# 136 columns in the weighted sums by differences of logits, an earlier count, and two kv steps one period later

## The chip, the cores and the metric

The kernel runs on one core of a Trainium2 chip. The metric is the device time in microseconds of one launch. The engines that matter here are TensorE (PE, matrix products), VectorE (DVE), ScalarE (ACT), GpSimd (POOL) and SyncE (SP), whose queue issues nearly all DMAs.

## The reference

Two layers follow one another: attention over a pooled key-value image, and a mixture of eight low-rank adapters, of which each token takes the best two. There are 4 batches of 12,288 tokens with 128 channels.

```python
kv_pool = kv.reshape(B, H // r, r, W // r, r, C).mean(axis=(2, 4))     # r = 4: 768 keys a batch
k = v = kv_pool.reshape(B, -1, C) @ w_sr
a = softmax(q @ k.T / sqrt(C))
x = (a @ v).reshape(B * S, D)

logits = x @ w_gate                                    # E = 8
topk = np.argpartition(-logits, 2, axis=1)[:, :2]
w = softmax(logits[topk])
out = x + sum(w[k] * (x @ A[topk[k]]) @ B[topk[k]])    # rank 16
```

Which two adapters are taken and their weights depend on differences of logits alone.

## The kernel before

**Tiling.** The 49,152 tokens are 96 chunks (NCH) of 512, 24 (CPB) to a batch. A chunk is 4 groups (NS) of 128 tokens, and a batch's 768 keys are 6 blocks (NJ) of 128. Two chunks are a pair.

**One chunk's way.** `scores` (L310) makes exp(scores) in three rounds: two products of 512 columns on PE into a score bank (L318, tile sg, two banks in turn), and one exponential on ACT (L319, tile tt). `weigh` (L321) multiplies them with the values: 24 products in two halves of 12, each with its own weight load of tt and as moving operand a row block of `vext` (L330, tile xps). A row of vext has VW = 137 columns: 128 value channels, the values times w_gate (8 logits, linear as the sum is), and a one, which gives the softmax's denominator. `normalise` (L334) takes the denominator's reciprocal (L337, kept in `rinv_all`), multiplies all 137 columns by it (L341, tile xn), and takes the sorted largest 8 of each token's logits (L348). xn is half of a tile that holds a pair, from a pool of five such tiles (`xpool`). `gate` on POOL (L350, five small instructions a pair) turns logits and largest two into tanh arguments, ACT takes the tanh, `send_gates` writes them to device memory by way of SP's queue (L418), and `load_gates` (L425) fetches them back broadcast over 128 partitions. Meanwhile PE transposes xn (L397, tile t_ps), DVE copies it (L408, xt), PE multiplies by A (L432, h_ps), DVE multiplies with the fetched gates (L435, ht), PE multiplies by B (L478, d_ps), DVE adds xn (L492, osb), and SP sends a pair (L510).

**Periods.** The whole order is written out by hand. A loop over c from 2 to 94 (L675) makes one period each: three rounds of scores for chunks ahead, `weigh(c-1)` in two halves, `normalise(c-1)`, the transposes of chunk c-2, and for chunks `lag` periods back (9 at first, then 8, 7 and from chunk 81 on 6) the product with A, and one period later the product with B and the output. Where the lag falls by one, one period handles two chunks. Engines work in program order, so what stands ahead in a queue delays what stands behind.

**Keys and values of the next batch.** `plan` (L270) spreads the work for batches 1 to 3 over the periods: loads of kv in 12 pieces, sums of rows and columns on POOL (L185, L189, L190), and three steps of three parts each: `pooled_transposed` (two transposes of the sums, L201), two periods later `values` (L205, products with `wext`, the 128 columns of w_sr and 8 of w_sr times w_gate), one later `keys` (L213). For batch 1 the steps begin in periods 9, 13 and 19; the sums they need are issued in periods 3 to 6, 8 to 10 and 12 to 16. `squares` and `ranges` (L251, L262) sum the values' squares on POOL and DVE, the latter in periods 32, 40, 56 and 80.

**The check of the ranges.** The kernel counts, over all tokens, denominators that lie in a safe range, and decides at the end by a flag whether a slow exact path (L905) must run. The first CUT = NCH - 8 = 88 chunks are counted by DVE in periods 89 to 91 (`count_ok`, L539), the values' ranges in period 92 (`values_ok`), and PE, ACT and DVE form the sum in period 93 (`count_sum`). In each of these periods the instruction stands in DVE's queue between L348 and L435. The other 8 chunks are counted by POOL after the last output addition (`tail_ok`, L562), on which one product (L569), a sum and the flag (L570, L572) follow.

Of the kernel before, what the change touches and what calls it, by code (L numbers as in the profile page):

```python
# [10 lines left out]
FP32 = mybir.dt.float32  # L11
# [4 lines left out]
AF = mybir.ActivationFunctionType  # L16
ALU = mybir.AluOpType
AX = mybir.AxisListType
# [3 lines left out]
def kernel(  # L22
# [10 lines left out]
    nc = tc.nc  # L33
    P = 128
    B, N, C = q.tensor.shape
    E = 8
# [3 lines left out]
    NJ = NKV // P  # L40
    NTOK = 512
    NS = NTOK // P
    VW = C + E + 1
    CPB = N // NTOK
    NCH = B * CPB
    scale = 1.0 / float(np.sqrt(C))
# [4 lines left out]
    const = ctx.enter_context(tc.tile_pool(name="const", bufs=1))  # L51
    kvpool = ctx.enter_context(tc.tile_pool(name="kvpool", bufs=4))
    keep = ctx.enter_context(tc.tile_pool(name="keep", bufs=1))
    qpool = ctx.enter_context(tc.tile_pool(name="qpool", bufs=3))
    ttpool = ctx.enter_context(tc.tile_pool(name="ttpool", bufs=4))
    xpool = ctx.enter_context(tc.tile_pool(name="xpool", bufs=5))
    run = ctx.enter_context(tc.tile_pool(name="run", bufs=3))
    small = ctx.enter_context(tc.tile_pool(name="small", bufs=3))
    ps_t = ctx.enter_context(tc.tile_pool(name="ps_t", bufs=1, space=bass.MemoryType.PSUM))
# [3 lines left out]
        name="ps_x", bufs=1, side="right", space=bass.MemoryType.PSUM))  # L63
# [90 lines left out]
    w_sr_sb = const.tile([P, P], FP32)  # L154
# [3 lines left out]
    wext = const.tile([P, C + E], FP32)  # L158
# [6 lines left out]
    mm(wg_ps, wT, w_gate_sb, start=True, stop=True)  # L165
    nc.vector.tensor_copy(wext[:, C:C + E], wg_ps)

    gw_all = keep.tile([P, 4, E, 2 * NS], F16, name="gw_all")
    rinv_all = keep.tile([P, NCH, NS], FP32, name="rinv_all")
    vss = keep.tile([P, 2 * B], FP32, name="vss")  # L170
    kpT, kfT, vext, sqsum = {}, {}, {}, {}
    kp_keep = keep.tile([P, B, NKV], FP32, name="kp_keep")
    for b in range(B):
        kpT[b] = kp_keep[:, b]
        if b >= 2:
            kfT[b], vext[b] = kfT[b - 2], vext[b - 2]
# [3 lines left out]
        nc.vector.memset(vext[b][:, :, C + E:VW], 1.0)  # L180


    def sum_row(b, t, d, eng):
# [8 lines left out]
    def stile(name):  # L192
        return ps_s.tile([P, 2, NTOK], FP32, tag="sg", name=name)
# [9 lines left out]
        nc.scalar.activation(kpT[b][:, 2 * t * P:2 * (t + 1) * P], kp_ps, AF.Copy)  # L203

    def values(b, t):  # L205
        v_ps = stile("v_ps")[:, 0, 0:2 * (C + E)].rearrange("p (g e) -> p g e", g=2)
        for g in range(2):
            j = 2 * t + g
            mm(v_ps[:, g], kpT[b][:, j * P:(j + 1) * P], wext, start=(g == 0), stop=(g == 1),  # L209
               skip_group_check=True)  # L210
        nc.scalar.activation(vext[b][:, 2 * t:2 * t + 2, 0:C + E], v_ps, AF.Copy)

    def keys(b, t):  # L213

# [23 lines left out]
            nc.vector.tensor_copy(kfT[0][:, k], k_ps)  # L238

    def tile_values(t):  # L240
        v_ps = mtile([P, 2, C + E], name="v_ps")
        for g in range(2):
            j = 2 * t + g
            mm(v_ps[:, g], kpT[0][:, j * P:(j + 1) * P], wext, start=(g == 0), stop=(g == 1),
               skip_group_check=True)
        if t < NT - 1:
            nc.scalar.activation(vext[0][:, 2 * t:2 * t + 2, 0:C + E], v_ps, AF.Copy)
        else:
            nc.vector.tensor_copy(vext[0][:, 2 * t:2 * t + 2, 0:C + E], v_ps)

    def squares(b, t):  # L251

        v = vext[b][:, 2 * t:2 * t + 2, 0:C + E]
        sq = keep.tile([P, 2, C + E], FP32, name=f"sq{b}") if t == 0 else small.tile(
            [P, 2, C + E], FP32, tag="sq", name="sq", bufs=1)
        nc.gpsimd.tensor_tensor(sq, v, v, op=ALU.mult)
        if t == 0:
            sqsum[b] = sq
        else:
            nc.gpsimd.tensor_tensor(sqsum[b], sqsum[b], sq, op=ALU.add)  # L260

    def ranges(b):  # L262
        nc.vector.tensor_reduce(vss[:, b:b + 1], sqsum[b][:, :, 0:C], axis=AX.XY, op=ALU.add)
        nc.vector.tensor_reduce(vss[:, B + b:B + b + 1], sqsum[b][:, :, C:C + E], axis=AX.XY,
                                op=ALU.add)


# [2 lines left out]
    def plan(b):  # L270
        c0 = CPB * (b - 1)
        if b == 1:
            at = [2, 2, 3, 4, 5, 5, 6, 8, 9, 9, 11, 13]
            sm = [3, 5, 6, 8, 9, 10, 12, 14, 16]
            st = [9, 13, 19]
        else:
            at = [-11, -9, -7, -5, -5, -3, -1, 1, 1, 3, 5, 7]
            sm = [-3, -1, 1, 3, 5, 7, 9, 11, 13]
            st = [4, 10, 16]
        for i, k in enumerate(at):  # L280
            loads.setdefault(c0 + k, []).append((b, i // 4, i % 4))
# [23 lines left out]

    tt, xps, xpair, xn, gw, gin, xT, hg, hgT, hps = {}, {}, {}, {}, {}, {}, {}, {}, {}, {}
    garg = {}
    GRP = GROWS // NTOK

    def scores(c, r):  # L310
# [10 lines left out]
    def weigh(c, h, banks=None):  # L321
# [5 lines left out]
        for j in range(h * NH, (h + 1) * NH):  # L327
            for s in range(NS):
                o = xps[c][:, s // 2, (s % 2) * VW:(s % 2 + 1) * VW]
                mm(o, tt[c][:, j, s * P:(s + 1) * P], vext[b][:, j, 0:VW],  # L330
                   start=(j == 0 and s % 2 == 0), stop=(j == NJ - 1 and s % 2 == 1),
                   skip_group_check=True)

    def normalise(c):  # L334
        ri = rinv_all[:, c]
        xv = xps[c][:, :, 0:2 * VW].rearrange("p b (s v) -> p b s v", v=VW)
        nc.vector.reciprocal(ri.rearrange("p (b s) -> p b s", b=2), xv[:, :, :, VW - 1])  # L337
        if c % 2 == 0:
            xpair[c // 2] = xpool.tile([P, 2 * NS, VW], FP32, tag="xn", name="xn")
        xn[c] = xpair[c // 2][:, (c % 2) * NS:(c % 2 + 1) * NS]  # L340
        nc.vector.tensor_tensor(  # L341
            xn[c].rearrange("p (b s) v -> p b s v", b=2), xv,
            ri.rearrange("p (b s) -> p b s", b=2).unsqueeze(3).broadcast_to([P, 2, 2, VW]),
            op=ALU.mult)
        if c % 2 == 0:
            gin[c // 2] = small.tile([P, 2 * NS, 8], FP32, tag="top", name="top")
        for s in range(NS):
            nc.vector.max(gin[c // 2][:, (c % 2) * NS + s], xn[c][:, s, C:C + E])  # L348
# [287 lines left out]
    warm(2)  # L636
    scores(0, 1)
    tile_values(1)
    scores(1, 1)
    weigh(0, 0)  # L640
# [16 lines left out]

    NQ = NCH // GRP

# [15 lines left out]
    for c in range(2, NCH - 1):  # L675
        b, k = divmod(c, CPB)
# [24 lines left out]
        prep_step(c)  # L701
        if c == CUT + 5:
            count_sum(0)
# [40 lines left out]
        name="ps_e", bufs=1, reuse_waits="tile", space=bass.MemoryType.PSUM))  # L744
# [57 lines left out]
    q_ = n // 2  # L802

    top = small.tile([P, 2 * NS, 8], FP32, tag="top", name="top")
    top4, top5 = top[:, 0:NS], top[:, NS:2 * NS]
    pair = xpool.tile([P, 2 * NS, VW], FP32, tag="xn", name="xn")
    xn[n - 1], xn[n] = pair[:, 0:NS], pair[:, NS:2 * NS]
    arg4, msk4, arg5, msk5 = (
        small.tile([P, NS, E], FP32, tag=f"r{i}", name=f"r{i}", bufs=1) for i in range(4))
    def tops4(c, top, y):  # L810
        ri = rinv_all[:, c]
        xv = y[:, :, 0:2 * VW].rearrange("p b (s v) -> p b s v", v=VW)
        nc.vector.reciprocal(ri.rearrange("p (b s) -> p b s", b=2), xv[:, :, :, VW - 1])
        nc.vector.tensor_tensor(
            xn[c].rearrange("p (b s) v -> p b s v", b=2), xv,
            ri.rearrange("p (b s) -> p b s", b=2).unsqueeze(3).broadcast_to([P, 2, 2, VW]),
            op=ALU.mult)
        for s in range(NS):
            nc.vector.max(top[:, s], xn[c][:, s, C:C + E])
# [11 lines left out]
        name="ps_f", bufs=1, side="right", space=bass.MemoryType.PSUM))  # L831
# [73 lines left out]
    with tc.If(bad_v != 0):  # L905
# [4 lines left out]
        e = big2[:, 0:NKV]  # L910
# [115 lines left out]
```

## Time and profile before

| | us |
|---|---|
| three runs | 378.99, 379.06, 381.55 |
| median | 379.06 |
| profiled execution | 378.6 |
| its span, first to last instruction | 376.8 |
| DVE busy in it | 300.4 |
| ACT busy in it | 310.1 |

In the profile, a row of a group names line, engine, operation and tiles, then busy time and mean duration, then the engine's idle time just before and what ended it. In a timeline the columns are start, duration, engine, line, operation, tiles, count, and in brackets the idle time before with its releaser. A matmul's duration there includes the way through the array; the distance between starts is what it costs in a stream. In the chain of waits the columns are start, duration, engine, tile and line.

### The profile page before, as it was taken

The numbers are of one execution on the slowest core, as the hardware profiler recorded it, in microseconds if no ns is written. First come the engines' busy times: TensorE is split into PE (matmuls) and PEld (weight loads), VectorE is DVE, ScalarE is ACT, GpSimd is POOL, SyncE is SP. The second block draws the span as 40 slices with busy tenths as digits, with TensorE's granted clock in tenths as the row PEclk, the third lists the DMA queues.
The fourth block names the chain that finished last, engine by engine and source line by source line (L and its number), as shares of the span: only waits on it lengthen the run. The fifth ranks groups of instructions, "written<-read, shape, count | busy, mean of one in ns | idle before, by whom it ended". The sixth has DMA issues, their size and how long they took to land.

```text
span 376.8 us, 10584 instructions
## 1 busy us (share of the span) xinstructions
PE 359.5 (95%) x3943; PEld 265.0 (70%) x3943; DVE 300.4 (80%) x950; ACT 310.1 (82%) x391; POOL 225.1 (60%) x375
## 2 busy tenths in 40 slices
PE   4889999999999999999999999999999999999983
PEld 1446767777777677777777777777776767776772
DVE  3784557888888788788888888888888898889983
ACT  1569999898898898988988898898888888888752
POOL 1013799979699887755679687755434234242244
PEclk9999999999999999999999999999999999999998
DMA  8998999999999999999999999998788699654325
GB/s 260 402 363 202 307 295 331 319 285 303 286 341 318 273 293 328 232 312 317 301 294 370 289 313 308 234 305 262 235 221 259 201 257 242 184 141 142 115 85 198
DMA packets 95593, 101.00 MB, mean 268 GB/s; under 512 B 58804, under 2 KB 59060, under 8 KB 95540
## 3 DMA queue, kind: packets, MB, share of 16 engines
q1 hardware_dynamic: 94068, 100.11, 94.5%
q8 instruction: 31, 0.51, 0.6%
q10 hardware_dynamic: 1472, 0.20, 0.3%
q14 instruction: 22, 0.18, 0.2%
HBM read 62.33 MB, written 25.90 MB: 234 GB/s over the span
## 4 chain that ended last, share of the span: by engine, by line
PE 78%; DVE 7%; POOL 7%; DMA 4%; issue 1%; ACT 1%; ACTq 0%; SPq 0%; POOLq 0%; DVEq 0%
PE xps L330 32%; PE sg L318 28%; PE d_ps L478 5%; PE t_ps L397 5%; PE h_ps L432 4%; DMA b_f<-in_moe_B_dram 3%; POOL kvt L185 2%; DMA kvt<-in_kv_dram 2%; DVE xn L341 2%; DVE ht L435 1%; PE v_ps L209 1%; DVE kvt L185 1%; POOL q L107 1%; POOL kvt L189 1%; PE kp_ps L201 1%
## 5 line engine op out<-in xcount | busy, mean ns | idle before, releaser
L319 ACT ACTIVATE tt<-sg 128x1024 f16<-128x1024 f32 x288 | 277.6, 1022 | 37.9 <-PE sg L318 37.0
L318 PE MATMUL sg<-qT,kfT 128*128 128x512 f16 x576 | 170.1, 379 | 0.4 <-ACT qT L585 0.3
L330 PEld LDWEIGHTS <-tt 128*128 128x128 f16 x2304 | 147.7, 98 | 28.5 <-DVE xn L341 18.6
L330 PE MATMUL xps<-vext,tt 128*128 128x137 f16 x2256 | 166.5, 223 | 0.3 <-DVE xn L341 0.2
L492 DVE TENSOR_TENSOR osb<-d_ps,xn 128x512 f32<-128x512 f32 x85 | 58.7, 691 | 30.0 <-PE d_ps L478 29.7
L357 POOL TENSOR_TENSOR arg<-xn,top 128x64 f32<-128x64 f32 x47 | 14.7, 313 | 102.0 <-DVE top L348 86.2
L341 DVE TENSOR_TENSOR xn<-xps,rinv_all 128x548 f32<-128x548 f32 x94 | 68.4, 728 | 3.3
L318 PEld LDWEIGHTS <-kfT 128*128 128x128 f16 x576 | 49.2, 98 | 24.1 <-issue 0.6
L185 POOL TENSOR_TENSOR kvt<-kvt 128x1024 f32<-128x1024 f32 x27 | 63.6, 2357 | 2.6 <-PE sg L318 2.5
L107 POOL CAST q<-q 128x1024 f16<-128x1024 f32 x45 | 46.8, 1041 | 24.8 <-DMA q<-in_q_dram 24.6
L435 DVE SCALAR_TENSOR_TENSOR ht<-ge,h_ps 128x512 bf16<-128x512 f16 x87 | 58.5, 672 | 1.5 <-PE sg L318 1.0
L478 PEld LDWEIGHTS <-ht 128*128 128x128 bf16 x368 | 27.3, 97 | 24.9 <-DVE ht L435 4.5
L348 DVE MAX8 top<-xn 128x8 f32<-128x8 f32 x376 | 35.1, 156 | 6.2
L408 DVE COPY xt<-t_ps 128x512 bf16<-128x512 bf16 x92 | 36.7, 399 | 0.0
L397 PE MATMUL t_ps<-id_bf,xn 128*128 128x128 bf16 x376 | 36.3, 219 | 0.0
L478 PE MATMUL d_ps<-b_bf,ht 128*128 128x128 bf16 x340 | 32.9, 219 | 1.0 <-DVE ht L435 0.9
L432 PE MATMUL h_ps<-xt,a_bf 128*128 128x512 bf16 x87 | 33.0, 379 | 0.1
L337 DVE RECIPROCAL rinv_all<-xps 128x4 f32<-128x4 f32 x94 | 17.1, 182 | 14.6 <-PE xps L330 12.3
L397 PEld LDWEIGHTS <-xn 128*128 128x128 bf16 x376 | 25.9, 98 | 0.3
L360 POOL TENSOR_SCALAR msk<-msk 128x64 f32<-128x64 f32 x47 | 20.1, 428 | 4.1
L361 POOL TENSOR_TENSOR arg<-arg,msk 128x64 f32<-128x64 f32 x47 | 15.0, 319 | 3.9
L359 POOL TENSOR_TENSOR arg<-arg,msk 128x64 f32<-128x64 f32 x47 | 15.0, 319 | 3.7
(147 smaller groups left out, 220.8 us busy)
## 6 DMA issues: line engine op xcount, KB each, us to landing
kvt<-in_kv_dram SPq DMA_DIRECT2D x48, 512.0 KB
q<-in_q_dram SPq DMA_DIRECT2D x46, 512.0 KB
out_dram<-osb SPq DMA_DIRECT2D x44, 512.0 KB
ge<-g_h SPq DMA_DIRECT2D x45, 256.0 KB
out_dram<-osb SPq DMA_DIRECT2D x8, 256.0 KB
q<-in_q_dram SPq DMA_DIRECT2D x1, 1024.0 KB
qT<-q SPq DMA_TRANSPOSE x46
g_h<-g_sb SPq DMA_DIRECT2D x45, 16.0 KB
```

The source lines that it names most:

```text
L107: nc.gpsimd.tensor_copy(q16[i], q32[i].rearrange("p k n -> p (k n)"))
L185: eng.tensor_tensor(v[:, 0], v[:, 0], v[:, d], op=ALU.add)
L318: mm(sg[:, k], kfT[b][:, j * P:(j + 1) * P], qc, start=True, stop=True)
L319: nc.scalar.activation(tt[c][:, 2 * r:2 * r + 2], sg, AF.Exp, bias=0.0, scale=scale)
L330: mm(o, tt[c][:, j, s * P:(s + 1) * P], vext[b][:, j, 0:VW], start=(j == 0 and s % 2 == 0), stop=(j == NJ - 1 and s % 2 == 1), skip_group_ ...
L341: nc.vector.tensor_tensor(xn[c].rearrange("p (b s) v -> p b s v", b=2), xv, ri.rearrange("p (b s) -> p b s", b=2).unsqueeze(3).broadcast_t ...
L397: mm(columns(t_ps, c, s), src[:, s], id_bf, is_transpose=True, start=(s == 0), stop=(s == NS - 1), skip_group_check=True)
L408: nc.vector.tensor_copy(to, t_ps)
L432: mm(h_ps, a_bf, xT[c], start=True, stop=True)
L435: nc.vector.scalar_tensor_tensor(hgT[c].rearrange("p (k a) t -> p k (a t)", k=2), gE[c // 2][:, h:h + NS // 2].rearrange("p a t k -> p k ( ...
L478: mm(dps[c][:, s], columns(hgT[c], c, s), b_bf, start=(s == 0 and fresh), stop=(s == NS - 1), skip_group_check=True)
L492: nc.vector.tensor_tensor(osb[:, lo:hi], d, xn[c][:, lo:hi, 0:C], op=ALU.add)
```

## The change

Seven differences to the last logit take the place of eight logits, so a row of vext has VW = 136 columns. The products of the values use a new matrix `wv`, made at the start on DVE: w_sr's 128 columns and seven differences of the gate's columns. The eighth logit is a zero that stands in the last column of xn from the start (a fill by POOL); the normalisation writes 135 columns. The five tiles of xpool become five slices of one tile, used in turn. Batch 1's first two steps begin in periods 10 and 14 instead of 9 and 13, with their later parts. CUT is NCH - 15 = 81, which moves the count by DVE, the values' ranges and the sum from periods 89 to 93 to periods 82 to 86; the count by POOL at the end covers 15 chunks, 60 columns instead of 32.

```diff
+    G = E - 1
-    VW = C + E + 1
+    VW = C + G + 1
...
-    xpool = ctx.enter_context(tc.tile_pool(name="xpool", bufs=5))
...
+    wv = const.tile([P, C + G], FP32)
+    nc.vector.tensor_copy(wv[:, 0:C], w_sr_sb)
+    nc.vector.tensor_scalar(wv[:, C:C + G], wext[:, C:C + G], wext[:, C + G:C + E], None,
+                            op0=ALU.subtract)
...
-            mm(v_ps[:, g], kpT[b][:, j * P:(j + 1) * P], wext, start=(g == 0), stop=(g == 1),
+            mm(v_ps[:, g], kpT[b][:, j * P:(j + 1) * P], wv, start=(g == 0), stop=(g == 1),
...
-            st = [9, 13, 19]
+            st = [10, 14, 19]
...
+    xn_all = keep.tile([P, 5, 2 * NS, VW], FP32, name="xn_all")
+    nc.gpsimd.memset(xn_all[:, :, :, C + G:VW], 0.0)
...
-            xpair[c // 2] = xpool.tile([P, 2 * NS, VW], FP32, tag="xn", name="xn")
+            xpair[c // 2] = xn_all[:, c // 2 % 5]
...
-            xn[c].rearrange("p (b s) v -> p b s v", b=2), xv,
-            ri.rearrange("p (b s) -> p b s", b=2).unsqueeze(3).broadcast_to([P, 2, 2, VW]),
+            xn[c][:, :, 0:C + G].rearrange("p (b s) v -> p b s v", b=2), xv[:, :, :, 0:C + G],
+            ri.rearrange("p (b s) -> p b s", b=2).unsqueeze(3).broadcast_to([P, 2, 2, C + G]),
...
-    CUT = NCH - 8
+    CUT = NCH - 15
...
-    pair = xpool.tile([P, 2 * NS, VW], FP32, tag="xn", name="xn")
+    pair = xn_all[:, q_ % 5]
```

More of the change, by code (lines that the diff above doesn't have):

```diff
@@ L179 @@
         vext[b] = keep.tile([P, NJ, 160], F16, name=f"vext{b}")
-        nc.vector.memset(vext[b][:, :, C + E:VW], 1.0)
+        nc.vector.memset(vext[b][:, :, C + G:VW], 1.0)
     def sum_row(b, t, d, eng):
@@ L205, in values @@
     def values(b, t):
-        v_ps = stile("v_ps")[:, 0, 0:2 * (C + E)].rearrange("p (g e) -> p g e", g=2)
+        v_ps = stile("v_ps")[:, 0, 0:2 * (C + G)].rearrange("p (g e) -> p g e", g=2)
         for g in range(2):
             j = 2 * t + g
-            mm(v_ps[:, g], kpT[b][:, j * P:(j + 1) * P], wext, start=(g == 0), stop=(g == 1),
+            mm(v_ps[:, g], kpT[b][:, j * P:(j + 1) * P], wv, start=(g == 0), stop=(g == 1),
                skip_group_check=True)
-        nc.scalar.activation(vext[b][:, 2 * t:2 * t + 2, 0:C + E], v_ps, AF.Copy)
+        nc.scalar.activation(vext[b][:, 2 * t:2 * t + 2, 0:C + G], v_ps, AF.Copy)
     def keys(b, t):
@@ L240, in tile_values @@
     def tile_values(t):
-        v_ps = mtile([P, 2, C + E], name="v_ps")
+        v_ps = mtile([P, 2, C + G], name="v_ps")
         for g in range(2):
             j = 2 * t + g
-            mm(v_ps[:, g], kpT[0][:, j * P:(j + 1) * P], wext, start=(g == 0), stop=(g == 1),
+            mm(v_ps[:, g], kpT[0][:, j * P:(j + 1) * P], wv, start=(g == 0), stop=(g == 1),
                skip_group_check=True)
         if t < NT - 1:
-            nc.scalar.activation(vext[0][:, 2 * t:2 * t + 2, 0:C + E], v_ps, AF.Copy)
+            nc.scalar.activation(vext[0][:, 2 * t:2 * t + 2, 0:C + G], v_ps, AF.Copy)
         else:
-            nc.vector.tensor_copy(vext[0][:, 2 * t:2 * t + 2, 0:C + E], v_ps)
+            nc.vector.tensor_copy(vext[0][:, 2 * t:2 * t + 2, 0:C + G], v_ps)
     def squares(b, t):
-        v = vext[b][:, 2 * t:2 * t + 2, 0:C + E]
-        sq = keep.tile([P, 2, C + E], FP32, name=f"sq{b}") if t == 0 else small.tile(
-            [P, 2, C + E], FP32, tag="sq", name="sq", bufs=1)
+        v = vext[b][:, 2 * t:2 * t + 2, 0:C + G]
+        sq = keep.tile([P, 2, C + G], FP32, name=f"sq{b}") if t == 0 else small.tile(
+            [P, 2, C + G], FP32, tag="sq", name="sq", bufs=1)
         nc.gpsimd.tensor_tensor(sq, v, v, op=ALU.mult)
@@ L263, in ranges @@
         nc.vector.tensor_reduce(vss[:, b:b + 1], sqsum[b][:, :, 0:C], axis=AX.XY, op=ALU.add)
-        nc.vector.tensor_reduce(vss[:, B + b:B + b + 1], sqsum[b][:, :, C:C + E], axis=AX.XY,
+        nc.vector.tensor_reduce(vss[:, B + b:B + b + 1], sqsum[b][:, :, C:C + G], axis=AX.XY,
                                 op=ALU.add)
@@ L814, in tops4 @@
         nc.vector.tensor_tensor(
-            xn[c].rearrange("p (b s) v -> p b s v", b=2), xv,
-            ri.rearrange("p (b s) -> p b s", b=2).unsqueeze(3).broadcast_to([P, 2, 2, VW]),
+            xn[c][:, :, 0:C + G].rearrange("p (b s) v -> p b s v", b=2), xv[:, :, :, 0:C + G],
+            ri.rearrange("p (b s) -> p b s", b=2).unsqueeze(3).broadcast_to([P, 2, 2, C + G]),
             op=ALU.mult)
```

## The prediction

> **What bounds the kernel now.** I read the page first, then busy time by stage, the chain of waits in order of time, the groups by line with their shapes, and last the timelines of TensorE (PE), VectorE (DVE), GpSimd (POOL) and the DMA queue (SP) round each place that the change touches.
>
> ```profile
> span 376.8 us, 10584 instructions
> ...
> PE 359.5 (95%) x3943; PEld 265.0 (70%) x3943; DVE 300.4 (80%) x950; ACT 310.1 (82%) x391; POOL 225.1 (60%) x375
> ```
>
> ```profile
> core 0: us, PE busy (x) PEld busy (x) DVE busy (x) ACT busy (x) POOL busy (x), PEclk, DMA share, GB/s
> 75.00:104.00 29.00, 29.00 (x331) 22.29 (x330) 24.07 (x81) 25.85 (x34) 22.69 (x35) 1.00 1.13 292
> 104.00:133.00 29.00, 28.23 (x324) 21.32 (x322) 24.10 (x78) 24.70 (x31) 25.67 (x38) 1.00 1.10 310
> 200.00:250.00 50.00, 50.00 (x568) 37.83 (x566) 42.28 (x138) 44.46 (x57) 39.78 (x55) 1.00 1.13 295
> 309.00:326.00 17.00, 17.00 (x196) 12.66 (x194) 14.92 (x50) 15.11 (x18) 7.32 (x18) 1.00 0.90 225
> 344.00:360.00 16.00, 15.16 (x179) 11.07 (x178) 14.73 (x52) 12.11 (x16) 3.88 (x12) 1.00 0.34 113
> ```
>
> The first number after each stage is its length. PE is full in the middle, but the last but one column says that the DMA engines are full as well (a share over 1 is overlapping packets), until 250 us. In the last stage DMA is free and DVE has 14.73 of 16 us.
>
> A busy PE may still be padded, so I looked at the chain. One period of it, from one chunk's weighing to the next:
>
> ```profile
> 161.18 0.72 PE xps L330 x12
> 161.90 0.43 PE sg L318 x2
> 162.34 0.22 PE d_ps L478 x4
> 162.56 0.72 PE xps L330 x12
> 163.28 0.22 PE t_ps L397 x4
> 163.50 0.43 PE sg L318 x2
> 163.93 0.22 PE h_ps L432
> 164.15 0.43 PE sg L318 x2
> 164.58 0.72 PE xps L330 x12
> ```
>
> Each piece begins where the one before it ends: 3.40 us, all of it matmul issue, so here a shorter matmul is a shorter period. 24 of its matmuls are the weighted sums, at 0.72 / 12 = 60.0 ns.
>
> **One column less.** The 512-column products take 0.43 / 2 = 215 ns, 0.42 ns per column; the 128-column ones 0.22 / 4 = 55 ns. From 55 ns, 9 columns more at 0.42 make 58.8 ns for 137 and 58.4 for 136, but 137 is issued at 60.0: the odd length seems to be rounded up. So the column is worth between 0.42 ns and 60.0 - 58.4 = 1.6 ns per matmul. I take 0.8, nearer to the lower end, since 0.22 and 0.72 are rounded themselves. A period gains 24 x 0.8 = 19 ns, 94 periods 1.8 us.
>
> The Trainium skill's page "TensorE: Matmul & The Clock Gate" (section "Wait — 56ns, not 53.3ns?") gives warm spacing as N / 2.4 + 2.5 ns: 59.6 ns for 137 and 59.2 for 136, so 0.42 ns each; by it the whole gain would be half of mine, and the 60.0 of the chain is a little above its 59.6.
>
> ```profile
> L330 PE MATMUL xps<-vext,tt 128*128 128x137 f16 x2256 | 166.5, 223 | 0.3 <-DVE xn L341 0.2
> L330 PEld LDWEIGHTS <-tt 128*128 128x128 f16 x2304 | 147.7, 98 | 28.5 <-DVE xn L341 18.6 <-ACT tt L319 0.3
> L341 DVE TENSOR_TENSOR xn<-xps,rinv_all 128x548 f32<-128x548 f32 x94 | 68.4, 728 | 3.3
> ...
> L492 DVE TENSOR_TENSOR osb<-d_ps,xn 128x512 f32<-128x512 f32 x85 | 58.7, 691 | 30.0 <-PE d_ps L478 29.7
> ```
>
> The normalisation goes from 548 to 540 elements. 36 elements more than L492 cost it 37 ns, so 8 fewer are 8 ns per chunk: shown only where DVE bounds, say 10 periods, 0.1 us. The 135 columns of the value products, their copies, squares and ranges differ by one or two columns in a few dozen instructions: nothing.
>
> **The two steps.** A step's first half is two transposes (L201) that need POOL's sums:
>
> ```profile
> 54.98 0.20 PEld L201 LDWEIGHTS kp_ps<-id_f,kvt 128*128 128x128 f32 x2 [0.35 <-POOL kvt L190]
> ...
> 70.03 0.20 PEld L201 LDWEIGHTS kp_ps<-id_f,kvt 128*128 128x128 f32 x2 [0.52 <-POOL kvt L190]
> ```
>
> In periods 9 and 13 PE stands 0.35 and 0.52 us for POOL. A period later both sums are some 3 us old, and both waits go: 0.87 us. Values and keys move along; the steps issue no DMA, so nothing moves in SP's or POOL's queue. The kv buffer that a step frees is wanted again only for batch 2's loads, from period 19 on. What is late next is the subject of the next part.
>
> **Who takes the early gain back.** Chunk 20's gate weights reach DVE by DMA:
>
> ```profile
> 122.36 0.59 SPq L425 DMA_DIRECT2D ge<-g_h  x1
> ```
>
> ```profile
> 127.87 0.22 DVE L348 MAX8 top<-xn 128x8 f32<-128x8 f32 x2
> 129.10 0.69 DVE L435 SCALAR_TENSOR_TENSOR ht<-ge,h_ps 128x512 bf16<-128x512 f16 x1 [1.02 <-PE sg L318]
> ```
>
> ```profile
> 128.48 0.59 PE L318 MATMUL sg<-qT,kfT 128*128 128x512 f16 x2
> 129.85 0.40 PE L478 MATMUL d_ps<-b_bf,ht 128*128 128x128 bf16 x4 [0.77 <-DVE ht L435]
> ```
>
> DVE stands 1.02 us before this product. The releaser named, a score matmul, isn't among its inputs; the other input is the gate load issued 6 us before, so I take the wait to be the DMA's. PE's scores were issued by 128.48 + 0.43 = 128.91 and d_ps at 129.85: 0.94 us lost. Since DMA engines that never idle deliver at a time set by the bytes ahead, and the change takes no byte out, this load should land near 129 again. Then whatever PE gains before it is only waited out: the 0.87 us, and about 27 periods of 19 ns, 0.5 us; 1.4 us in all. What remains of the column is the 64 periods after it: 64 x 24 x 0.8 ns = 1.2 us. If the load does come earlier with its issue, the 1.4 us stay.
>
> **The count.** Five pieces of DVE work move from periods 89 to 93 to 82 to 86. They stand in DVE's queue ahead of ht (L435), on which d_ps on PE waits, and behind that PE's whole queue. The same place shows what an insertion costs in a period of this length, where the ranges of batch 2 are summed:
>
> ```profile
> 224.15 0.40 DVE L263 TENSOR_REDUCE vss<-sq 128x1 f32<-128x256 f32 x1
> 224.46 0.16 DVE L264 TENSOR_REDUCE vss<-sq 128x1 f32<-128x16 f32 x1
> 224.54 0.68 DVE L435 SCALAR_TENSOR_TENSOR ht<-ge,h_ps 128x512 bf16<-128x512 f16 x1
> ```
>
> ```profile
> 224.70 0.59 PE L318 MATMUL sg<-qT,kfT 128*128 128x512 f16 x2
> 225.28 0.40 PE L478 MATMUL d_ps<-b_bf,ht 128*128 128x128 bf16 x4
> ```
>
> ht starts 224.54 - 224.15 = 0.39 us later than without them; PE loses 225.28 - (224.70 + 0.43) = 0.15. So about 0.24 us of an insertion is free. Where the count stands now it is dearer:
>
> ```profile
> 344.90 0.59 PE L318 MATMUL sg<-qT,kfT 128*128 128x512 f16 x2
> 345.84 0.38 PE L478 MATMUL t_ps<-b_bf,ht 128*128 128x128 bf16 x4 [0.34 <-DVE xt L408]
> ...
> 349.19 0.59 PE L318 MATMUL sg<-qT,kfT 128*128 128x512 f16 x2
> 349.94 0.40 PE L478 MATMUL d_ps<-b_bf,ht 128*128 128x128 bf16 x4 [0.16 <-DVE ht L435]
> ...
> 352.92 0.59 PE L318 MATMUL sg<-qT,kfT 128*128 128x512 f16 x2
> 353.58 0.40 PE L478 MATMUL d_ps<-b_bf,ht 128*128 128x128 bf16 x4
> ```
>
> Against 0.43 after the scores, PE loses 0.51, 0.32 and 0.23 us in three periods, 1.06 in all. The first has two chunks to finish and would lose some 0.1 anyway: 0.95 us go.
>
> ```profile
> L543 DVE SCALAR_TENSOR_TENSOR ok<-rinv_all,ok 128x352 f32<-128x352 f32 x1 | 0.5, 506 | 0.0
> ...
> L546 DVE TENSOR_REDUCE flags<-ok 128x1 f32<-128x352 f32 x1 | 0.5, 501 | 0.0
> ...
> L563 POOL TENSOR_SCALAR ok<-rinv_all 128x32 f32<-128x32 f32 x1 | 0.3, 292 | 0.0
> ```
>
> In the new place the pieces have 324 of 352 columns. The two of 0.5 us delay ht by about 0.4 each and so cost 0.15 each, as the ranges do; the third, three small instructions that together delay ht by nearly 0.5 and cost 0.23 now, again 0.23; the first and last are under the free 0.24. That is 0.53 us back, net gain 0.4 us. Its bounds: nothing free at all, some 1.7 us of insertions exposed; or all hidden, 0.95 us gained. I stay with the ranges' row, which has the same queue and the same period. The sum over partitions (one PE product and an ACT copy) moves unchanged.
>
> **The end.** The last 15 chunks instead of 8 are counted by POOL after everything: three instructions on 60 columns instead of 32, at 0.29 us now. Bounds: no more than now, or in proportion, 3 x 0.29 x 28 / 32 = 0.76 us. They stand on the chain's last piece, with one product and one sum behind them. I take 0.3, as a fixed part must be in 0.29 us for 32 elements a lane.
>
> **Cover.** DVE gets two operations more at the start, ahead of its first kv sum, and POOL a fill of 40 columns; DVE there still waits for kv from DMA and POOL for q, so nothing; uncovered, each is a few tenths.
>
> **The sum**, on the profiled execution of 378.6 us (span 376.8 and 1.8 around it; 0.12% under the median of 379.06): -1.2 column, -0.1 normalisation, -0.4 count, +0.3 end, early gain 0: -1.4 us, 377.2. Carried to the median, 379.06 - 1.4 = **377.7 us**.
>
> **The rivals.**
>
> 1. *The early gain stays* (25%): the gate load lands earlier because it is issued earlier. For it: SP's own time for the transposes ahead of it stretches and might shrink again. Against: DMA share 1.10. -1.4 more: 376.3.
> 2. *The column is worth little* (15%): weight loads pace these pairs. The skill's same page (section "Back-to-back issue gap") says that a stream of weight load and matmul at N = 128 is spaced by both, at about 81 ns. Against: each weighted sum has its own load of 98 ns on PEld's row and is still issued every 60, and the 128-column products every 55, so length shows. Column 0: 378.9; column 0.42: 378.2.
> 3. *DVE becomes the bound in periods 82 to 86* (12%), slower. For it: DVE has 14.92 of 17.00 us just before, so 0.42 free per 3.40, part of it in the wrong place. If the 1.7 us of insertions are exposed and the late stalls come back for the doubled chunks, the count costs 1.7 instead of gaining 0.4: 379.8. It decides once ht is later than its free 0.24 us and the lateness is handed to the next period; the ranges' row speaks against it, since osb waits for d_ps again.
> 4. *The normalised chunks' buffer is treated as one* (3%): five pool tiles become slices of one, and a chunk's transposes could come to wait for the next chunk's normalisation. The price is about 1.1 us in each of 94 periods, some 480 us. Against it: pairs share a tile now, and t_ps (163.28 in the chain) starts without waiting for the other half's normalisation.
> 5. *The change doesn't do what it says* is small: logits reach the gate only as differences, so 7 and a zero serve as well as 8.
>
> The forecast has 45%. The range of 8 in 10 takes rival 1 at the lower end, with a dearer odd column (1.6 ns) below it, and rival 3 at the upper: 375.4 to 379.8. 1% is 3.8 us, about what a measurement of this kernel can tell from no change: faster needs 375.2, rival 1 with the dear column and a hidden count, 8%; slower is rival 4 and little else, 4%; within 1% 88%.
>
> **What would show it.** The chain's groups of 12 at 0.71 us and a period of 3.38; no wait of L201 on POOL; the stall before chunk 20's ht longer by about the time by which its period begins earlier; no stall at d_ps where the count was, small ones in periods 83 to 85. Wrong it would be if ht doesn't wait near 129 us (rival 1), if xps still takes 0.72 in a period of 3.40 (2), or if periods 82 to 87 grow by over 0.3 us each (3).

## The result

The changed kernel takes 375.88 us (median of 8 runs, 375.38 to 376.86) where the kernel before, on the same chip, takes 379.02: a ratio of 0.991, with a 95% interval from 0.9886 to 0.9934. The forecast of 377.7 had the direction right and less than half of the size: 1.4 us were expected, 3.1 came. The profiled execution took 375.4 us against 378.6. Below, a median leaves out single executions that were over 1.5% longer than the fastest of their kernel (one each in three kernels), and a ratio with its interval is taken from the rest against executions of the kernel before on the same chip.

The page of the changed kernel, its first line, the busy times and the groups that answer to those shown of before:

```profile
span 373.6 us, 10589 instructions
...
PE 356.5 (95%) x3942; PEld 262.8 (70%) x3943; DVE 299.6 (80%) x952; ACT 309.4 (83%) x391; POOL 225.6 (60%) x376
...
L338 PE MATMUL xps<-vext,tt 128*128 128x136 f16 x2256 | 164.7, 223 | 0.3 <-DVE xn_all L349 0.2
...
L349 DVE TENSOR_TENSOR xn_all<-xps,rinv_all 128x540 f32<-128x540 f32 x94 | 67.7, 721 | 3.3
...
L443 DVE SCALAR_TENSOR_TENSOR ht<-ge,h_ps 128x512 bf16<-128x512 f16 x87 | 58.5, 673 | 1.4 <-DMA ge<-g_h 1.0
```

Line numbers from here on are 6 to 8 higher in the changed kernel: the weighted sums L330 are L338, the scores L318 are L326, ht's L435 is L443, d_ps's L478 is L486, the steps' L201 is L207. PE is 3.0 us less busy, DVE, ACT and POOL hardly change, and the last row names what the page of before didn't: of 1.4 us in which DVE stood before its ht products, 1.0 was for the gate weights' DMA (the row of before has 1.5, with 1.0 put down to a score product).

The chain of waits of the changed kernel over one period (start, duration, engine, tile, line):

```profile
157.00 0.22 PE d_ps L486 x4
157.22 0.71 PE xps L338 x12
157.93 0.22 PE t_ps L405 x4
158.15 0.43 PE sg L326 x2
158.59 0.22 PE h_ps L440
158.80 0.43 PE sg L326 x2
159.23 0.71 PE xps L338 x12
159.94 0.43 PE sg L326 x2
160.38 0.22 PE d_ps L486 x4
```

From d_ps to d_ps it is 160.38 - 157.00 = 3.38 us, and a group of twelve weighted sums takes 0.71. The distance between starts in the trace, to more digits, was 60.0 ns for 137 columns in the kernel before (2072 of 2112 pairs) and is 59.2 for 136; an ordinary period went from 3.397 to 3.378 us.

To see where the 3.1 us lie, I measured in every profile when PE begins each period (the first weighted sum of a chunk), and cut the loop in three: periods 2 to 20, which hold the two steps; 20 to 33, which hold the stall before chunk 20's ht; 33 to 95, which hold the count. In us:

| kernel | 2 to 20 | 20 to 33 | 33 to 95 |
|---|---|---|---|
| before | 61.70 | 46.69 | 219.91 |
| before, a second profile | 61.81 | 46.81 | 219.89 |
| changed | 60.46 | 46.41 | 218.25 |
| changed, a second profile | 60.46 | 46.46 | 218.25 |

So the gain is 1.3 us early, 0.3 in the middle and 1.65 late, less 0.3 at the end: period 95 starts 17.35 us before the end in the kernel before and 17.66 in the changed one. That makes 2.9 of the 3.2 by which the span is shorter; the rest lies ahead of period 2, which starts anywhere from 30.9 to 34.8 us over the profiles of this case, so that one profile says nothing about it.

### The profile page after: what moved, and what is told of

It reads as the page before. It is cut to its first block, busy times and chain, and to the rows that moved or that the text cites. A ratio compares the mean times of both kernels' runs of the same rounds, so it can differ in the third digit from the quotient of the medians.

```text
span 373.6 us, 10589 instructions
## 1 busy us (share of the span) xinstructions
PE 356.5 (95%) x3942; PEld 262.8 (70%) x3943; DVE 299.6 (80%) x952; ACT 309.4 (83%) x391; POOL 225.6 (60%) x376
## 4 chain that ended last, share of the span: by engine, by line
PE 83%; DVE 5%; POOL 4%; DMA 3%; ACT 2%; issue 1%; SPq 0%; POOLq 0%; DVEq 0%
PE xps L338 33%; PE sg L326 30%; PE t_ps L405 5%; PE d_ps L486 5%; PE h_ps L440 4%; DMA kvt<-in_kv_dram 2%; DMA ge<-g_h 2%; ACT tt L327 1%; PE v_ps L215 1%; POOL osb L495 1%; DVE xn_all L349 1%; DVE osb L500 1%; DVE ht L443 1%; DVE kvt L191 1%; PE k_ps L240 1%
## 5 line engine op out<-in xcount | busy, mean ns | idle before, releaser
L326 PE MATMUL sg<-qT,kfT 128*128 128x512 f16 x576 | 170.2, 379 | 0.5 <-ACT qT L593 0.3
L338 PEld LDWEIGHTS <-tt 128*128 128x128 f16 x2304 | 146.1, 98 | 28.4 <-DVE xn_all L349 18.1
L338 PE MATMUL xps<-vext,tt 128*128 128x136 f16 x2256 | 164.7, 223 | 0.3 <-DVE xn_all L349 0.2
L500 DVE TENSOR_TENSOR osb<-d_ps,xn_all 128x512 f32<-128x512 f32 x85 | 58.7, 691 | 28.7 <-PE d_ps L486 27.7
L365 POOL TENSOR_TENSOR arg<-xn_all,top 128x64 f32<-128x64 f32 x47 | 14.5, 308 | 99.6 <-DVE top L356 80.2
L349 DVE TENSOR_TENSOR xn_all<-xps,rinv_all 128x540 f32<-128x540 f32 x94 | 67.7, 721 | 3.3
L326 PEld LDWEIGHTS <-kfT 128*128 128x128 f16 x576 | 49.1, 98 | 24.4 <-issue 1.5
L443 DVE SCALAR_TENSOR_TENSOR ht<-ge,h_ps 128x512 bf16<-128x512 f16 x87 | 58.5, 673 | 1.4 <-DMA ge<-g_h 1.0
L486 PEld LDWEIGHTS <-ht 128*128 128x128 bf16 x368 | 27.0, 98 | 24.6 <-DVE ht L443 5.7
L356 DVE MAX8 top<-xn_all 128x8 f32<-128x8 f32 x376 | 35.1, 156 | 6.3
L405 PE MATMUL t_ps<-id_bf,xn_all 128*128 128x128 bf16 x376 | 36.3, 219 | 0.0
L486 PE MATMUL d_ps<-b_bf,ht 128*128 128x128 bf16 x340 | 32.9, 219 | 0.8 <-DVE ht L443 0.7
L405 PEld LDWEIGHTS <-xn_all 128*128 128x128 bf16 x376 | 25.9, 98 | 0.3
```

What stands on the lines that cost most here:

```text
L326: mm(sg[:, k], kfT[b][:, j * P:(j + 1) * P], qc, start=True, stop=True)
L338: mm(o, tt[c][:, j, s * P:(s + 1) * P], vext[b][:, j, 0:VW], start=(j == 0 and s % 2 == 0), stop=(j == NJ - 1 and s % 2 == 1), skip_group_ ...
L349: nc.vector.tensor_tensor(xn[c][:, :, 0:C + G].rearrange("p (b s) v -> p b s v", b=2), xv[:, :, :, 0:C + G], ri.rearrange("p (b s) -> p b ...
L405: mm(columns(t_ps, c, s), src[:, s], id_bf, is_transpose=True, start=(s == 0), stop=(s == NS - 1), skip_group_check=True)
L443: nc.vector.scalar_tensor_tensor(hgT[c].rearrange("p (k a) t -> p k (a t)", k=2), gE[c // 2][:, h:h + NS // 2].rearrange("p a t k -> p k ( ...
L486: mm(dps[c][:, s], columns(hgT[c], c, s), b_bf, start=(s == 0 and fresh), stop=(s == NS - 1), skip_group_check=True)
```

## Each part alone

The first question was which part brings what. Three kernels take the kernel before with one part each.

**The steps alone.**

```diff
-            st = [9, 13, 19]
+            st = [10, 14, 19]
```

> The kernel before with batch 1's first two steps in periods 10 and 14, nothing else. Both theories: no wait of L201 on POOL (0.35 and 0.52 us before). Theory 'fixed' (chunk 20's gate load lands near 129 us whatever PE does, since the DMA engines are never idle): the wait of ht for it grows from 1.02 to about 1.9 us and the time stays within 0.2 us of before. Theory 'follows' (the load lands earlier because SP comes to it earlier): the wait stays near 1.0 us, ht starts 0.9 us earlier, and the time is 0.9 us shorter.

Measured: 378.45 us, ratio 0.9992 (0.9977 to 1.0007). Periods 2 to 20 take 60.79 us, 0.9 less than before: both waits on POOL are gone. The timeline of DVE shows what became of it:

```profile
129.79 0.69 DVE L435 SCALAR_TENSOR_TENSOR ht<-ge,h_ps 128x512 bf16<-128x512 f16 x1 [1.29 <-DMA ge<-g_h]
```

The idle time before chunk 20's ht grew from 1.02 to 1.29 us. Some 0.3 of the 0.9 was waited out, which lies between the two theories, and the 0.6 left is too little for the timing to tell from none.

**The count alone.**

```diff
-    CUT = NCH - 8
+    CUT = NCH - 15
```

> The kernel before with the count in periods 82 to 86 over 81 chunks, and 60 columns for POOL at the end. By the prediction's terms: 0.95 us of stalls at d_ps go from periods 90 to 93, about 0.5 us come in periods 83 to 86, the end is 0.3 us longer: 0.1 us faster. The rival (DVE the bound in periods 82 to 86): periods 82 to 87 together 1.7 us longer, the kernel over 1 us slower.

Measured: 378.48 us, ratio 0.9975 (0.9953 to 0.9997). Periods 33 to 95 take 219.43 us instead of 219.91: 0.5 less.

**The column alone** (the changed kernel with the steps and CUT of before).

```diff
-            st = [10, 14, 19]
+            st = [9, 13, 19]
...
-    CUT = NCH - 15
+    CUT = NCH - 8
```

> The changed kernel with the steps in periods 9 and 13 and the count in 89 to 93 as before: only the column, the differences of logits and the one buffer are left of the change. If an odd length is rounded up: groups of 12 weighted sums 0.71 us, periods 3.377 instead of 3.397, 94 x 20 ns = 1.9 us shorter if all of it stays, 1.3 us if theory 'fixed' eats what is gained before 129 us. If a column is worth 0.42 ns: 1.0 or 0.6 us shorter.

Measured: 378.71 us (378.06 to 382.44), ratio 1.0013 (0.9983 to 1.0043). From period 33 on it gains 1.0 us (218.92); 62 periods of 19 ns would be 1.2, but period 93, with the count's sum still in it, takes 4.01 us instead of 3.87. Ahead of that it gains nothing: 62.03 us for periods 2 to 20, more than the kernel before. The weight loads of the steps' transposes in PE's timeline say why:

```profile
56.21 0.20 PEld L207 LDWEIGHTS kp_ps<-id_f,kvt 128*128 128x128 f32 x2 [1.07 <-POOL kvt L196]
...
71.09 0.20 PEld L207 LDWEIGHTS kp_ps<-id_f,kvt 128*128 128x128 f32 x2 [0.42 <-POOL kvt L196]
```

The two waits were 0.35 and 0.52 in the kernel before, and are 1.07 and 0.42 here. POOL's sums didn't come earlier, so a PE that is ahead stands there longer. But most of it is where POOL began: its first sum starts 9.56 us after period 2 here and 8.93 in the kernel before. Of the 0.72 us more in period 9, PE came 0.12 earlier, and the sum ended 0.61 later. After that the stall before chunk 20's ht (1.16 us) takes its share as well.

**138 columns.** The kernel before with one column more, which nothing reads.

```diff
-    VW = C + E + 1
+    VW = C + E + 2
```

> The kernel before with a 138th column, a second column of ones that nothing reads except the normalisation (552 elements). If an odd number of columns is rounded up to the next even one, the period stays 3.397 us and the time that of before within 0.2 us; if each column costs 0.42 ns, the period is 3.407 and the time 0.9 us longer.

Measured: 379.56 us, ratio 1.0016 (0.9989 to 1.0043), too wide to tell no change from 0.9 us; the profile decides. Two groups of its page:

```profile
L330 PE MATMUL xps<-vext,tt 128*128 128x138 f16 x2256 | 166.5, 223 | 0.3 <-DVE xn L341 0.2
...
L341 DVE TENSOR_TENSOR xn<-xps,rinv_all 128x552 f32<-128x552 f32 x94 | 68.9, 733 | 3.3
```

PE's busy time for 2256 products is 166.5 us, to the digit what 137 columns cost, and the period is 3.397. So the 138th column is free, and the step from 137 to 136 gains what two columns cost by the 0.42 ns of the longer products: 0.83 ns per product, where the forecast took 0.8.

## All of it, and the parts together

The profiled execution of the changed kernel and of the kernel before could each have been an accident, so both ran again unchanged.

> The changed kernel once more, for a second profile. If its 3.1 us are the kernel's own, it is again 3 us under before, its first pair of chunks is weighed near 24.0 us, and chunk 20's ht starts near 127 us. If the first profile was a lucky start of the loads, ht starts between 128.5 and 130 us as in the other profiles, and the profiled time is 1 to 2 us longer.

> The kernel before once more, for a second profile: how far the start of the first transposed load (28.3 us in the first profile) and of chunk 20's ht (129.1 us) move from run to run. Theory 'fixed': the two move together, within 1 us of a distance of 100.5 us.

Measured: 376.04 us, ratio 0.9913 (0.9882 to 0.9943), and one profile of the kernel before, 379.6 us. Both second profiles agree with the first within 0.12 us in each of the three stretches of the table above. In the changed kernel chunk 20's ht starts at 127.46 us, as in its first profile (127.31). In the kernel before it starts 100.8 and 101.0 us after the first transposed load, within the expected 1 us of 100.5; in the changed kernel this distance is 99.5 and 99.6.

**Column and steps, without the count** (the changed kernel with CUT back at NCH - 8).

```diff
-    CUT = NCH - 15
+    CUT = NCH - 8
```

> The changed kernel with the count back in periods 89 to 93 over 88 chunks. If the parts add up as they were measured alone, it is as long as before (steps 0.6 us shorter, column 0.4 longer). If the count alone is what it seems (0.5 us by the profiles) and the rest of the 3.1 us comes from column and steps together, 2.5 us shorter than before.

Measured: 376.83 us, ratio 0.9942 (0.9923 to 0.9961). The stretches are 60.47, 46.37 and 218.90 us. So the early 1.3 is there with column and steps together, while each alone showed no gain in time that its interval tells from none. (Without the count's move, period 93 takes 4.01 us here as well, so beside the column the count is worth 0.65 us, 218.90 - 218.25.) With the steps a period later, PE waits for POOL in neither (the row of the steps' weight loads has 0.0 us of idle time instead of 0.9 in the kernel before and 1.5 in the column alone), so the column's shorter periods are kept as well.

**Which step holds the column back.** Two kernels put the steps of the changed kernel back, both or the first alone.

```diff
-            st = [10, 14, 19]
+            st = [9, 13, 19]
```

> The changed kernel with both steps back in periods 9 and 13. If the steps are worth only their own waits of the kernel before (0.87 us), the time is 0.9 over the changed kernel, 376.9. If the shorter products make PE wait longer at the steps, as in the profile of the column alone (idle 1.35 us in period 9 and 0.46 in period 13, against 0.39 and 0.56 in the kernel before), then all that the column has won before period 13 is waited out there: from the second chunk's weighing to period 20's some 62.0 us as in the kernel before, instead of 60.5, and from period 33 to 95 the full 218.25 of the changed kernel; the time is 1.5 to 2.2 over it, 377.5 to 378.2.

```diff
-            st = [10, 14, 19]
+            st = [9, 14, 19]
```

> The changed kernel with only the first step back in period 9, the second in period 14. If the first step's wait is what swallows the early gain, period 9 has 1.1 us more of idle time than in the changed kernel, the stretch from the second chunk's weighing to period 20's is near 61.5 us, and the time some 1 us over the changed kernel, 377.0. If it is the second step's, or if that one wait in one profile was an accident, period 9 has some 0.2 us more as in the kernel before, that stretch is 60.7 and the time within 0.4 us of 376.0.

Measured: 377.06 us, ratio 0.9935 (0.9911 to 0.996), and 376.91 us, ratio 0.9926 (0.9898 to 0.9955). Against the changed kernel's 375.88 and 376.04 that is 1.0 to 1.2 and 0.9 to 1.0 us, but the intervals of the ratios overlap with the changed kernel's. With the first step back, its page groups have the wait:

```profile
L207 PEld LDWEIGHTS kp_ps<-id_f,kvt 128*128 128x128 f32 x18 | 1.8, 141 | 0.7 <-POOL kvt L196 0.7
```

Periods 2 to 20 take 61.31 us, near the 61.5 expected of the first step as the culprit, with 0.7 us of wait instead of 1.1. With both steps back they take 60.80, and the same row has 0.1: in that profile POOL's first sum started 8.13 us after period 2, the earliest of all, and PE hardly waited. So the expected 62.0 was wrong as a fixed number. The wait at the old steps is between 0.1 and 1.5 us by when POOL gets going, and that differs by 1.2 us between the two profiles of the changed kernel (8.49 and 9.67 us). A period later the wait was zero in every profile, with POOL's start anywhere from 8.5 to 10.0 us. That is what the steps' move buys.

## Why the gate load did not take it back

The forecast let chunk 20's gate load land where it had landed, with the early gain waited out in front of it. The wait is still there in the changed kernel, and it is no longer than before; so the load came earlier too. DVE's and PE's timelines, and the issue on SP, of the changed kernel:

```profile
127.31 0.69 DVE L443 SCALAR_TENSOR_TENSOR ht<-ge,h_ps 128x512 bf16<-128x512 f16 x1 [0.98 <-DMA ge<-g_h]
```

```profile
126.72 0.59 PE L326 MATMUL sg<-qT,kfT 128*128 128x512 f16 x2
128.05 0.40 PE L486 MATMUL d_ps<-b_bf,ht 128*128 128x128 bf16 x4 [0.73 <-DVE ht L443]
```

```profile
121.56 0.80 SPq L433 DMA_DIRECT2D ge<-g_h  x1
```

The wait is 0.98 us against 1.02, and the load needs 127.31 - 121.56 = 5.8 us from issue to use where it needed 129.10 - 122.36 = 6.7. Two theories: its landing is set by the bytes ahead of it, or by what the compute had done by then. Three experiments move the load or the bytes.

**The gate loads one period earlier** (in the stage with lag 9, in the changed kernel; they then stand ahead of SP's transposes).

```diff
-        fetched[2 * p + 3 + {9: 3 + (lag(2 * p + 3) > 8), 8: 2, 7: 2, 6: 1}[lag(2 * p + 1)]] = p
+        fetched[2 * p + 3 + {9: 2 + (lag(2 * p + 3) > 8), 8: 2, 7: 2, 6: 1}[lag(2 * p + 1)]] = p
```

> The changed kernel with the gate loads of the stage with a lag of 9 issued one period earlier. If chunk 20's ht waits for its gate load in a queue that is always full, the load stands one period ahead of the turned queries, lands some 3 us earlier, the wait of 1.0 us near 129 goes, and the kernel is about 0.9 us shorter than the changed one, unless another transfer becomes late. If the wait is for something else, nothing changes.

Measured: 376.53 us, ratio 0.9927 (0.9899 to 0.9954), no better than the changed kernel. The load is issued 2.7 us earlier, ahead of the transposes:

```profile
118.90 0.56 SPq L433 DMA_DIRECT2D ge<-g_h  x1
119.57 2.12 SPq L117 DMA_TRANSPOSE qT<-q  x1
```

```profile
126.77 0.67 DVE L443 SCALAR_TENSOR_TENSOR ht<-ge,h_ps 128x512 bf16<-128x512 f16 x1
```

DVE no longer stands before chunk 20's ht, which starts 1.1 us earlier against period 2 than in the changed kernel; the load's issue came 3.2 us earlier by the same measure. How much earlier the load landed can't be read here, since nobody waits for it. The gain doesn't last: periods 20 to 33 shrink by 0.7 to 45.75 us, and periods 33 to 95 grow by 0.45 to 218.70, with a new stall of 0.35 us in period 58.

**One kv load behind the gate load**, in the changed kernel and in the kernel before.

```diff
-            at = [-11, -9, -7, -5, -5, -3, -1, 1, 1, 3, 5, 7]
+            at = [-11, -9, -7, -5, -5, -3, -1, 1, 3 if b == 2 else 1, 3, 5, 7]
```

> The changed kernel with one edit: of the two 512 KB loads of batch 2's kv that stand in SP's queue some 6 us ahead of chunk 20's gate load, the second is issued two periods later, behind that gate load. If the landing of the gate load is set by the bytes ahead of it, 512 KB less at about 300 GB/s bring it 1.7 us earlier, more than the 1.0 us that DVE waits for it in the changed kernel: the idle time before chunk 20's ht falls under 0.3 us, chunk 20's product comes 0.7 to 1.0 us earlier after the head, and the time is 375.0 to 375.4 against 376.0, unless a later gate load takes the wait over. If the landing is set by something else (the arrival of the first loads, or what PE had done by then), the wait stays at 1.0 us and the time within 0.3 us of 376.0.

> The kernel before with the same single edit: one 512 KB load of batch 2's kv issued two periods later, behind chunk 20's gate load. If bytes ahead set the landing, the stall of 0.9 to 1.1 us before chunk 20's ht falls under 0.3 us and the time by 0.7 to 1.0 us, to 378.0 to 378.7 against about 379.2, with the columns and the steps of the kernel before; PE then reaches chunk 20 some 97 us after the second chunk's weighing instead of 98. If not, stall and time stay as in the kernel before. With both runs: if the stall goes in both, the changed kernel keeps the whole 1.4 us that its PE has won by then, and the distance between the two is 1.4 early, 1.0 of the column later and 0.5 of the count, less 0.4 at the end: 2.5 us and some more for the first periods.

Measured: 376.24 us, ratio 0.9934 (0.9909 to 0.9959), and 378.58 us, ratio 0.9976 (0.9954 to 0.9997). DVE's timeline of the changed kernel with the later load, chunks 20 and 22:

```profile
127.61 0.69 DVE L443 SCALAR_TENSOR_TENSOR ht<-ge,h_ps 128x512 bf16<-128x512 f16 x1 [0.28 <-DMA ge<-g_h]
...
135.93 0.69 DVE L443 SCALAR_TENSOR_TENSOR ht<-ge,h_ps 128x512 bf16<-128x512 f16 x1 [1.12 <-DMA ge<-g_h]
```

And of the kernel before with it:

```profile
128.48 0.67 DVE L435 SCALAR_TENSOR_TENSOR ht<-ge,h_ps 128x512 bf16<-128x512 f16 x1
...
136.87 0.69 DVE L435 SCALAR_TENSOR_TENSOR ht<-ge,h_ps 128x512 bf16<-128x512 f16 x1 [0.99 <-DMA ge<-g_h]
```

In both, the wait of 1.0 us before chunk 20 falls (to 0.28, and to none) and stands whole before chunk 22, which waited for nothing in the changed kernel and in the kernel before and whose load is now the one behind the moved 512 KB. The landing goes by what stands ahead of the load: that part of the forecast was right. Whether by its bytes or by its place in SP's queue is not separated, since SP also issues chunk 20's gate load 2.0 to 2.2 us earlier against period 2 in these two runs.

In the changed kernel the time does not fall (376.24), and periods 2 to 33 take 107.28 us instead of 106.9, since the next load is just as late; the expectation's "unless a later gate load takes the wait over" is what happened. The kernel before does gain by its medians, 378.58 against 379.38 on that chip, as the expectation had it. But its profile doesn't show the gain: periods 2 to 33 take 108.25 us instead of 108.39 and 108.62. The wait is thus not chunk 20's own; it looks as if the whole DMA stream runs about 1 us behind PE up to here.

So the stream itself must have come earlier. I added up the bytes moved since the first instruction, and took the times from the start of period 2. The 38th megabyte is through at 91.4 and 91.5 us in the two profiles of the changed kernel, at 91.9 and 92.1 in those of the kernel before, 0.4 to 0.7 later; the 39th takes 4.4 us in the one and 5.4 in the other. Busy time by stage, the 5 us from 93 us after period 2 on, with the rate in the last column; the kernel before:

```profile
core 0: us, PE busy (x) PEld busy (x) DVE busy (x) ACT busy (x) POOL busy (x), PEclk, DMA share, GB/s
...
124.20:129.20 5.00, 4.88 (x55) 3.44 (x53) 3.28 (x14) 4.48 (x6) 4.75 (x8) 1.00 1.16 167
```

The changed kernel, and the count alone:

```profile
123.70:128.70 5.00, 4.27 (x53) 3.10 (x50) 3.21 (x10) 4.44 (x6) 4.75 (x8) 1.00 0.88 264
```

```profile
125.90:130.90 5.00, 4.85 (x56) 3.50 (x55) 3.91 (x13) 4.49 (x6) 4.75 (x8) 1.00 0.89 272
```

The stream has a hole here in every profile, in which SP's transposes and the gate load itself move, but it is deeper in some: 167, 161, 159 and 210 GB/s in the kernel before, its second profile, the column alone and the steps alone; 264, 268 and 270 in the changed kernel, its second profile and column with steps. The count alone and 138 columns have neither the shorter products nor the moved steps and yet 272 and 285. So the deep hole is not a property of the kernel before, and its absence not a merit of the change alone. DVE's timeline with 138 columns, where the wait before chunk 20's ht is under 0.15 us and ht starts 96.95 us after period 2, against 97.92 and 98.14 in the kernel before:

```profile
128.57 0.69 DVE L435 SCALAR_TENSOR_TENSOR ht<-ge,h_ps 128x512 bf16<-128x512 f16 x1
```

Where the deep hole is missing without the change, periods 2 to 33 take 107.4 to 107.5 us; with it, in the kernel before, 108.4 and 108.6; in the changed kernel 106.9. The two kernels with a step back have the small hole too (265 and 241 GB/s) and take 107.5 and 107.4. Compared like with like, the early gain is thus 0.5 to 0.6 us, and the 1.5 to 1.7 of the profiles is this and a hole that costs 1 us less.

What fills the hole can be seen in part. In each of these profiles a packet of 16 KB of program code starts 90 to 91.4 us after period 2 and takes 1.0 us, where a 4 KB packet of data takes 0.16. Some 2 us later, for 0.9 to 1.0 us, nothing starts in the kernel before but single 4 KB packets, one every 0.16 us, while some 20 of the transposes' packets stand unfinished. The profile doesn't name a packet's engine; that these are what one engine had left over behind the code packet is inferred from the durations. A second code packet, of 8 KB, comes just ahead of the transposes' first packets in the changed kernel (92.0 and 91.9 us after period 2), where some of the transposes' packets do start in that time, and among their last ones in the kernel before (94.8 and 95.0), where the last packets of the gates' write then trail for 1.1 us instead of 0.3. But with 138 columns and in the count alone it comes late as well (94.3 and 94.4), and there the hole is small. What decides stays open; no run here moved a code packet without moving the rest.

## The prediction, step by step

- **The column** was right: 0.8 ns per product was taken and 0.83 measured, 1.2 us were expected after the stall and 1.0 came (column alone, periods 33 to 95). The reason held too: 137 columns cost what 138 do. The rule of the Trainium skill's page "TensorE: Matmul & The Clock Gate" (section "Wait — 56ns, not 53.3ns?") gives 59.2 ns for 136, as measured, and 59.6 for 137, where 60.0 was measured; 60.0 is what it gives for 138. Its section "Back-to-back issue gap", with about 81 ns for a weight load and matmul at N = 128, is not borne out by any run here: 55 ns for the 128-column products, and 59.2 to 60.0 for twelve weighted sums in a row, each with its own weight load. Rival 2 fell with it.
- **The normalisation** went from 728 to 721 ns, near the 8 ns that were read from the longer addition's row. Whether that is worth the 0.1 us of the sum no run shows.
- **The count** was right. PE's timeline of the changed kernel, in periods 84 to 86 and at the old place:

```profile
317.81 0.59 PE L326 MATMUL sg<-qT,kfT 128*128 128x512 f16 x2
318.46 0.40 PE L486 MATMUL d_ps<-b_bf,ht 128*128 128x128 bf16 x4
...
321.42 0.59 PE L326 MATMUL sg<-qT,kfT 128*128 128x512 f16 x2
322.00 0.40 PE L486 MATMUL d_ps<-b_bf,ht 128*128 128x128 bf16 x4
...
324.95 0.59 PE L326 MATMUL sg<-qT,kfT 128*128 128x512 f16 x2
325.54 0.40 PE L486 MATMUL d_ps<-b_bf,ht 128*128 128x128 bf16 x4
...
342.72 0.59 PE L326 MATMUL sg<-qT,kfT 128*128 128x512 f16 x2
343.22 0.38 PE L486 MATMUL t_ps<-b_bf,ht 128*128 128x128 bf16 x4
```

  Less the 0.43 of the scores, PE loses 0.22, 0.15 and 0.16 us where 0.15, 0.15 and 0.23 were taken, 0.53 together as the forecast had it, and 0.07 at the old place where it lost 1.06. The losses fall a period later than forecast, since the product with B follows its ht by a period. In 33 to 95 this makes 0.5 (count alone) to 0.65 us (changed kernel against column and steps), where 0.4 was taken. DVE is no bound there: rival 3 fell.
- **The end** cost 0.3 and 0.4 us in the two pairs of profiles (17.35 to 17.66 us from period 95 to the end, and 17.46 to 17.82), where 0.3 was taken. But over all profiles the kernels with the old CUT take 17.35 to 17.60 there and those with the new one 17.51 to 17.82, so the size is known only roughly. POOL's three instructions of the count grew from 0.88 us, start to end, to 1.08:

```profile
368.26 0.36 POOL L571 TENSOR_SCALAR ok<-rinv_all 128x60 f32<-128x60 f32 x1
368.59 0.36 POOL L572 TENSOR_SCALAR low<-rinv_all 128x60 f32<-128x60 f32 x1
369.03 0.31 POOL L573 TENSOR_TENSOR low<-low,ok 128x60 f32<-128x60 f32 x1
```

- **"Early gain 0"** was the step that failed. The forecast put it so: "this load should land near 129 again. Then whatever PE gains before it is only waited out". PE's own gain before it was sized well (1.4 forecast; 1.4 and 1.5 by the start of period 30), and that the landing goes by what stands ahead of the load held. But "near 129" was one profile's number and not a clock: ht, for which the landing sets the start, came 1.4 to 1.7 us earlier against period 2 in the changed kernel, with the same bytes ahead, of which 1.0 is the hole above. Against 138 columns and the count alone, whose hole is as small, it came 0.5 to 0.6 us earlier, and the wait is 0.98 us instead of 0.13 and 0.40; in that comparison 0.6 to 0.9 us of PE's gain is waited out, as the forecast said. Rival 1, which the forecast gave 25%, names what happened, with 376.3 us as its time. That it came so near to 375.9 is in part luck: its reason (SP issues the load earlier) covers only a part, since against period 2 the load's issue gained 0.4 to 0.7 us, and the 1.0 us of the hole was in no term of the forecast.
- **Rivals 4 and 5** showed nothing: the chunks' slices of one tile make nobody wait, as the unbroken period of 3.38 us shows. The 1.1 us a period that rival 4 was priced at stood on no row, and no run shows it.

No kernel tried here has a lower median than the changed one.

## What to carry to other kernels

Where PE waits for sums of a slower engine, a shorter product ahead of the wait only makes PE wait longer, and the wait itself can be worth more than one profile shows: moving the consumer a period back took away a wait of 0.1 to 1.5 us, and let the shorter products count. A DMA queue with a backlog is a bound of its own: the load that was moved behind the late one only handed the wait to the next. And a landing time read from one profile is not a constant to subtract from. A second profile of the same kernel did not show this (97.92 and 98.14 us after period 2); a neighbour with one edit elsewhere did (96.95 with 138 columns). So profile a neighbour as well before a term of the sum rests on a landing.

## What the runs showed of the hardware that was not expected

- A moving operand of 137 columns costs what 138 do (60.0 ns from start to start, 166.5 us busy for 2256 in both), and 136 cost 59.2.
- The DMA stream, with a full queue behind it, falls from some 300 to 160 GB/s for 5 us, at the same place in both profiles of the kernel before; a single 16 KB packet of program code takes 1.0 us shortly ahead of it, where a 4 KB packet of data takes 0.16.
- Period 2 began between 30.9 and 34.8 us after the first instruction over the profiles of this case, whose code ahead of it is nearly the same; the two profiles of the changed kernel differ by 0.1 us there, those of the kernel before by 0.6. This scatter is larger than the whole gain, so profiles were compared from period 2 on.
